# A transformer block on one core: projection and feed-forward products beside a value burst issued as four 32-column tiles, with the engine orders and banks written out as lists

## The chip, the core and the metric

The kernel runs on one core of a Trainium2 chip. The metric is device time in microseconds (us), from the first to the last instruction of one execution, the median of three runs. The engines named below are PE (TensorE, matmuls), PEld (TensorE's weight loads), ACT (ScalarE), DVE (VectorE), POOL (GpSimd) and SP (the engine that issues most DMAs).

## The reference

```python
# x: 2048 tokens x 1024; 32 query heads of 32, one key/value head (multi-query attention)
mod = (silu(c) @ w_mod)                                   # six vectors sa, ca, ga, sb, cb, gb
h = layernorm(x) * (1 + ca) + sa
q = h @ wq; k = h @ wk; v = h @ wv
p = softmax(q k^T * 32**-0.5)
x = x + ga * ((p v) @ wo)
h = layernorm(x) * (1 + cb) + sb
x = x + gb * ((silu(h @ w1) * (h @ w3)) @ w2)             # w1, w3: 1024 x 3584
```

## The kernel before, in words

**Attention.** Queries are cut into 8 blocks of 256 tokens, and the 32 heads into 8 groups of four. That makes 64 units (block, group), and each unit has 8 *steps*, one for each 256 keys: 512 steps in all. In step c the function `s_exp` issues one score burst on PE: 8 matmuls with 32 rows each, four at a time in the four row groups of the array, written `S<-QT,KT` in the profile. They fill four of the six score banks (tensor S6, `S` in the profile). Then ACT takes the exponential in two instructions of 128x1024 (`U<-S`), which write slot c mod 10 of U. The third burst back used the same banks, so that score burst c can only start once the first exponential of step c-1 is done.

When the 8 steps of a unit have their exponentials, `av` multiplies them with the values: 64 matmuls (`PB<-U,V`) of 128 rows and 32 columns, four at a time at `tile_position` (0, 0), (0, 32), (0, 64) and (0, 96), one head each. This is the *value burst*. The softmax's denominators are sums on DVE (`pairs`, `psum`: `PS<-U`, `PS<-PS`), followed by four matmuls with a matrix of ones (`md`, `PB<-PS,ONES`); DVE transposes, inverts and scales (`finish_av`).

**The rest of PE's work** consists of products with 128 rows and 128 columns: the query projection (`q_proj`, `PB<-HT,W`), the output projection (`wo`, `PB<-WO,QT`), the first feed-forward layer in 14 slabs of 256 columns per token block (`slab`, `PB<-QT,HT` and `PB<-QT,W`) and the second in four quarters (`quarter`, `PB<-W2S,HT`). Each instruction moves 256 or 512 columns of the moving operand. The feed-forward layers of token block n run during the attention of block n+1 and n+2; those of the last block run after the last step. During the attention all these products and the value burst share two PSUM banks (6 and 7, `PB`); the six score banks join them after the last exponentials. A group of nodes that fills a bank and the ones that empty it form a session (`Sess`), and the bank is free again when the last of them is done.

**The order.** `build` makes a graph of 7193 nodes, one for each small group of instructions (two 256-column products, 8 value matmuls, one DVE or ACT instruction, one DMA). Each PE node has a `mode`: "S" for a score burst, "A" for value and ones matmuls with 32 columns, "F" for the 128-column products. `Placer` (line 564) then places them: it keeps a planned time for each engine, and `choose` picks the ready node with the lowest due time, corrected by a row of the table `PLAN` (line 115) that holds for 8 steps: by how late a score burst may be, by how long value products and "F" products must stay apart after a score burst (`hold`), and by offsets per kind of node and engine. `bank_for` gives a session the bank that is free first. Within an engine instructions run in the order in which they were placed, and `emit` adds semaphore waits for the node's predecessors on other engines.

Of the kernel before, what the change touches and what calls it, by code (L numbers as in the profile page):

```python
# [8 lines left out]
P = 128  # L9
# [11 lines left out]
def play(e, call):  # L21
    return getattr(e, call[0])(*call[1], **call[2])  # L22

# [19 lines left out]
class Graph:  # L43
# [4 lines left out]
    def __init__(self, nc):  # L48
        self.nc = nc
        self.nodes = []  # L50
        self.last = {}
        self.readers = {}
        self.tag = None

    def op(self, eng, fn, dur, reads=(), writes=(), vt=0.0, mode=None, sess=None, post=0.05, waw=True, after=(),
# [27 lines left out]
        for key in writes:  # L83
            for p in self.readers.get(key, ()):
                if p is not n:
                    self._edge(p, n, False)
            if waw:
                for p in self.last.get(key, ()):
                    self._edge(p, n, True)
# [17 lines left out]
    def alias(self, new, old):  # L107
# [7 lines left out]
PLAN = [  # L115
    (0.15, 0.06, 0.0, 1, 2.5,
     {"-/pe": -103, "-/act": -50, "-/sp": 3, "an/dve": 282, "av/dve": -1, "k/pe": -256, "k/dve": -10, "kb/pe":
      -34, "kb/dve": 65, "ln/pe": -40, "ln/act": -38, "ln/dve": -35, "ln/pool": -168, "mc/dve": -131, "mc/sp":
      108, "mod/pe": 152, "mod/dve": -37, "out/sp": -203, "pair/dve": 33, "q/pe": -5, "q/dve": 85, "q/sp": 102,
      "quarter/pe": 283, "quarter/dve": -115, "quarter/sp": -6, "s/pe": -111, "s/act": 268, "slab/pe": -5,  # L120
      "slab/act": -109, "slab/dve": -124, "slab/sp": -92, "v/pe": 334, "v/dve": -2, "v/pool": 65, "wo/pool": 36,
      "wo/sp": 49}),
    (0.05, 0.0, 0.02, 1, 0.5,
     {"-/pe": -121, "-/dve": 5, "-/pool": 99, "an/dve": 28, "av/pe": -78, "av/dve": 293, "k/pe": -7, "k/dve": 5,
      "kb/pe": -3, "kb/dve": -7, "ln/pe": -135, "ln/act": -119, "ln/dve": 218, "ln/pool": 78, "mc/pe": -52,
      "mc/dve": -88, "mc/sp": 27, "mod/pe": -3, "mod/dve": -58, "pair/dve": 15, "q/pe": -194, "q/dve": 14,
      "quarter/dve": 169, "s/pe": -109, "s/act": 7, "sc/dve": -11, "slab/pe": -47, "slab/act": -3, "slab/dve":
      -201, "slab/sp": 35, "v/pe": 32, "v/dve": -164, "v/pool": 298, "wo/pe": -1, "wo/dve": 18, "wo/pool": 11,
      "wo/sp": 3}),
    (0.3, 0.16, 0.1, 0, 3.1,  # L130
     {"-/pe": -93, "-/act": 12, "-/dve": -31, "-/pool": -31, "an/dve": 150, "av/pe": 7, "av/dve": 140, "k/pe":
      32, "k/dve": 90, "kb/pe": 2, "kb/dve": -29, "ln/pe": -31, "ln/act": -6, "ln/dve": 351, "ln/pool": -30,
      "mc/pe": -4, "mc/dve": -69, "mc/sp": -137, "mod/dve": 45, "out/sp": -162, "pair/dve": 66, "q/dve": 67,
      "quarter/pe": -36, "quarter/sp": 1, "s/pe": -112, "s/act": 140, "sc/dve": -32, "slab/pe": 146, "slab/act":
      -146, "slab/dve": -120, "slab/sp": -5, "v/pe": 131, "v/pool": -72, "wo/dve": 100, "wo/pool": -3}),
    (0.12, 0.06, 0.3, 0, 3.0,
     {"-/pe": 23, "-/act": -86, "-/dve": -4, "an/dve": 63, "av/pe": -29, "av/dve": 40, "k/pe": 4, "kb/dve": -10,
      "ln/pe": -27, "ln/act": 2, "ln/pool": 220, "mc/pe": 152, "mc/dve": 120, "mc/sp": -35, "mod/pe": -220,
      "mod/dve": -16, "out/sp": -16, "q/dve": 7, "q/sp": -147, "quarter/pe": -153, "quarter/dve": -41,
      "quarter/sp": -39, "s/pe": 23, "s/act": 1, "sc/dve": 74, "slab/pe": -18, "slab/dve": 2, "slab/sp": 30,  # L140
      "v/pe": -5, "v/dve": 35, "v/pool": 168, "wo/pool": 2, "wo/sp": -85}),
    (0.12, 0.24, 0.1, 1, 0.8,
     {"-/pe": -90, "-/act": 54, "-/dve": -67, "-/pool": 131, "an/dve": 109, "av/pe": 17, "av/dve": -135,
      "k/dve": 56, "kb/dve": 4, "ln/pe": -27, "ln/act": 1, "ln/pool": -16, "mc/pe": 4, "mc/dve": 10, "mc/sp":
      -8, "mod/dve": -44, "out/sp": -171, "q/pe": -226, "q/dve": -34, "q/sp": -3, "quarter/pe": 37,
      "quarter/dve": 416, "quarter/sp": -122, "s/pe": 145, "s/act": 282, "sc/dve": -18, "slab/pe": 96,
      "slab/act": -104, "slab/dve": 17, "slab/sp": 60, "v/pool": 23, "wo/pe": -24, "wo/dve": -41, "wo/pool":
      -164, "wo/sp": -28}),
    (0.12, 0.2, 0.02, 1, 3.2,
     {"-/pe": 9, "-/act": 22, "-/dve": -30, "-/pool": 14, "an/dve": 85, "av/pe": -38, "av/dve": -130, "k/pe": 8,  # L150
      "k/dve": 63, "kb/dve": 1, "ln/pe": -5, "ln/act": 96, "ln/dve": 351, "ln/pool": -16, "mc/pe": -3, "mc/dve":
      -18, "mc/sp": -3, "mod/pe": 2, "mod/dve": -44, "out/sp": -301, "pair/dve": -20, "q/pe": -94, "q/dve": 65,
# [408 lines left out]
]  # L561


class Placer:

    SWITCH = {"F": 0.105, "S": 0.111, "A": 0.1155}
    LAT = {("dve", "pe"): 0.12, ("act", "pe"): 0.1, ("act", "dve"): 0.06}
    SEM = 0.06
    SPAN = 8

    def __init__(self, g, banks, later, plan):
# [249 lines left out]
def build(nc, x_in, wq_in, wk_in, wv_in, wo_in, w1_in, w3_in, w2_in, c_in, wmod_in, out, S, D, F):  # L821
# [803 lines left out]
    i = 0  # L1625
# [108 lines left out]
```

## Time and profile before

| what | value |
|---|---|
| median of 3 runs | 1130.08 us (1130.03 to 1130.63) |
| the profiled execution, its span | 1129.6 us, 34462 instructions |
| PE / PEld / DVE / ACT / POOL busy | 98% / 67% / 86% / 90% / 5% of the span |
| granted PE clock, mean | 0.998 |
| first score burst / last score burst / end | 30.06 / 1026.61 / 1129.6 us |
| DMA engines busy, by the queue's own packets | 66% of 16 engines' span |

The profiled execution's span stands 0.5 us under the median of the runs. Three parts follow each other: about 30 us of layer norm, transposes and first projections; about 997 us from the first score burst to the last, in which ACT works through 1024 exponentials while PE does everything else in between; and 103 us after the last score burst, in which PE works off what is left of block 6 and all of block 7.

### The profile page before, as it was taken

The numbers are of one execution on the slowest core, as the hardware profiler recorded it, in microseconds if no ns is written. First come the engines' busy times: TensorE is split into PE (matmuls) and PEld (weight loads), VectorE is DVE, ScalarE is ACT, GpSimd is POOL, SyncE is SP. The second block draws the span as 40 slices with busy tenths as digits, with TensorE's granted clock in tenths as the row PEclk, the third lists the DMA queues.
The fourth block names the chain that finished last, engine by engine and source line by source line (L and its number), as shares of the span: only waits on it lengthen the run. The fifth ranks groups of instructions, "written<-read, shape, count | busy, mean of one in ns | idle before, by whom it ended". The sixth has DMA issues, their size and how long they took to land.

```text
span 1129.6 us, 34462 instructions
## 1 busy us (share of the span) xinstructions
PE 1110.8 (98%) x15472; PEld 753.3 (67%) x15472; DVE 976.4 (86%) x1484; ACT 1017.2 (90%) x1155; POOL 51.5 (5%) x95
## 2 busy tenths in 40 slices
PE   8999999999999999999999999999999999999998
PEld 6643445666577766777577766776577756776887
DVE  7877899999899989998999899988999899987542
ACT  6899999999999999999999999999999999984110
POOL 4100000000000001000100001000100001000000
PEclk9999999999999999999999999999999999999999
DMA  9500368665697656865696577865597568677794
GB/s 345 184 2 2 113 184 225 192 183 164 141 245 203 190 141 179 243 192 155 151 269 192 166 184 179 237 193 155 129 274 207 157 172 209 195 223 217 222 249 154
DMA packets 374307, 209.45 MB, mean 185 GB/s; under 512 B 17552, under 2 KB 365968, under 8 KB 374160
## 3 DMA queue, kind: packets, MB, share of 16 engines
q1 hardware_dynamic: 373728, 207.11, 66.3%
q8 instruction: 122, 2.00, 0.8%
q14 instruction: 25, 0.20, 0.1%
q10 hardware_dynamic: 432, 0.13, 0.0%
HBM read 199.89 MB, written 4.19 MB: 181 GB/s over the span
## 4 chain that ended last, share of the span: by engine, by line
PE 73%; ACT 22%; DVE 2%; DMA 1%; issue 0%; SPq 0%; POOL 0%
PE PB L22 55%; ACT U L22 21%; PE S L22 19%; DMA W<-in_A_wq_dram 1%; ACT HT L22 1%; DVE ST L22 1%; DVE PS L22 1%; DVE HT L22 0%; SPq L22 0%; ACT XNB L22 0%; DVE KT L22 0%; DVE XNB L22 0%; POOL RS L22 0%; DVE QT L22 0%; DVE X L22 0%
## 5 line engine op out<-in xcount | busy, mean ns | idle before, releaser
L22 ACT ACTIVATE U<-S 128x1024 bf16<-128x1024 f32 x1024 | 961.7, 1154 | 7.2 <-PE S L22 5.1
L22 DVE TENSOR_TENSOR PS<-U 128x2048 bf16<-128x2048 bf16 x248 | 300.9, 1218 | 34.1 <-ACT U L22 30.9
L22 DVE TENSOR_TENSOR PS<-PS 128x1024 bf16<-128x1024 bf16 x304 | 268.3, 883 | 4.8
L22 PE MATMUL PB<-QT,W 128*128 128x256 bf16 x1824 | 226.7, 273 | 0.0
L22 PE MATMUL S<-QT,KT 32*128 32x256 bf16 x4096 | 203.7, 273 | 6.8 <-ACT U L22 3.3
L22 PEld LDWEIGHTS PB<-QT,W 128*128 128x128 bf16 x1824 | 167.5, 98 | 45.7 <-issue 27.6
L22 PE MATMUL PB<-W2S,HT 128*128 128x256 bf16 x1512 | 187.5, 273 | 0.0
L22 PEld LDWEIGHTS PB<-W2S,HT 128*128 128x128 bf16 x1512 | 138.2, 98 | 39.4 <-issue 23.6
L22 PEld LDWEIGHTS S<-QT,KT 32*128 32x128 bf16 x4096 | 60.8, 92 | 141.6 <-ACT U L22 137.7
L22 PE MATMUL PB<-U,V 128*32 128x256 bf16 x4096 | 132.3, 273 | 0.6 <-DVE QT L22 0.6
L22 PE MATMUL PB<-QT,HT 128*128 128x256 bf16 x928 | 117.0, 273 | 0.0
L22 PEld LDWEIGHTS PB<-U,V 128*32 128x32 bf16 x4096 | 105.7, 97 | 12.9 <-issue 8.0
L22 PE MATMUL PB<-HT,W 128*128 128x256 bf16 (+1 forms) x576 | 103.3, 320 | 1.1 <-DVE QT L22 0.5
L22 PEld LDWEIGHTS PB<-QT,HT 128*128 128x128 bf16 x928 | 85.4, 98 | 22.7 <-issue 13.3
L22 DVE SCALAR_TENSOR_TENSOR HT<-HT,PB 128x512 bf16<-128x512 bf16 x100 | 68.4, 684 | 18.0 <-ACT HT L22 17.6
L22 ACT ACTIVATE HT<-PB 128x512 bf16<-128x512 f32 (+1 forms) x102 | 71.4, 701 | 9.0 <-PE PB L22 8.2
L22 PEld LDWEIGHTS PB<-HT,W 128*128 128x128 bf16 x576 | 50.2, 98 | 38.8 <-issue 14.6
L22 DVE TENSOR_TENSOR HT<-HT,PB 128x512 bf16<-128x512 bf16 x100 | 68.2, 682 | 4.3 <-PE PB L22 3.1
L22 ACT ACTIVATE HT<-S 128x512 bf16<-128x512 f32 (+1 forms) x16 | 11.1, 702 | 59.7 <-PE S L22 59.6
L22 POOL TENSOR_SCALAR RS<-MV 128x1 f32<-128x1 f32 x32 | 14.2, 445 | 968.8 <-DVE MV L22 968.8
L22 PE MATMUL PB<-WO,QT 128*128 128x512 bf16 x224 | 55.4, 381 | 0.0
L22 PEld LDWEIGHTS PB<-WO,QT 128*128 128x128 bf16 x224 | 18.8, 97 | 24.6 <-issue 7.2
(119 smaller groups left out, 699.4 us busy)
## 6 DMA issues: line engine op xcount, KB each, us to landing
W<-in_B_w_dram SPq DMA_DIRECT2D x150, 512.0 KB, 5.0
W2S<-in_B_w_dram SPq DMA_DIRECT2D x28, 1792.0 KB, 8.3
HT<-in_B_w_dram SPq DMA_DIRECT2D x74, 512.0 KB, 5.0
W2S<-in_w_mod_dram SPq DMA_DIRECT2D x8, 1024.0 KB, 7.4
X<-in_A_x_dram SPq DMA_DIRECT2D x8, 512.0 KB, 6.6
out_dram<-X SPq DMA_DIRECT2D x7, 512.0 KB, 9.6
U<-in_B_w_dram SPq DMA_DIRECT2D x1, 3584.0 KB, 18.3
W2S<-in_B_w_dram SPq DMA_DIRECT2D x1, 3584.0 KB, 12.7
```

The lines of the kernel that those rows point to most:

```text
L22: return getattr(e, call[0])(*call[1], **call[2])
```

## The change

**Lists in place of the planner.** `Placer` and `PLAN` are gone. The class `Ordered` takes from the table `ORDER`, for each engine, the list of node numbers in the order in which it is to issue them, and from the string `BANKS` the bank of each session. It fixes nothing else: waits are still added from the graph's edges.

**Column tiles.** `Ordered.run` cuts PE's list at the score bursts. Where a piece between two score bursts holds at least one "A" node, all "F" nodes of that piece are marked (`narrow`), and `emit` passes their calls through `column_tiles`: each matmul with 128 weight columns and at least 256 moving columns becomes four matmuls with 32 weight columns each, which write 32 partitions each of the same bank, at the same four tile positions as the value burst. The piece after the last score burst holds the last value burst, so that all products after it are marked as well.

**Graph edges.** A write that does not order itself behind the last writer (`waw=False`) now keeps the edges that the first writer had.

```diff
+def column_tiles(calls):
+    r = []
+    for name, (dst, w, x), k in calls:
+        if name != "matmul" or w.shape[-1] != P or dst.shape[0] != P or len(w.shape) != 2 or x.shape[-1] < 256:
+            return calls
+        for h in range(4):
+            q = slice(32 * h, 32 * (h + 1))
+            r.append((name, (dst[q], w[:, q], x), dict(k, tile_position=(0, 32 * h))))
+    return r
...
         for key in writes:
-            for p in self.readers.get(key, ()):
-                if p is not n:
-                    self._edge(p, n, False)
+            before = [(p, False) for p in self.readers.get(key, ()) if p is not n]
             if waw:
-                for p in self.last.get(key, ()):
-                    self._edge(p, n, True)
+                before += [(p, True) for p in self.last.get(key, ())]
+                self.before[key] = before
+            else:
+                before += self.before.get(key, [])
+            for p, strong in before:
+                self._edge(p, n, strong)
...
-PLAN = [
-    (0.15, 0.06, 0.0, 1, 2.5,
...
+ORDER = {
+    "pe": """
+        31-35 23 36-47 25 48-52 65 53-57 28 27 105 122-132 74 133-137 96 76-77 148 168 177 113 157 115-118 107 195 108
...
+BANKS = (
+    "6676776677767767776767666667666776767776767767676767776677676676676777676776677667676666766767676776"
...
+        step = []
+        for i in self.order["pe"] + [None]:
+            if i is None or nodes[i].mode == "S":
+                if any(nodes[k].mode == "A" for k in step):
+                    self.narrow.update(k for k in step if nodes[k].mode == "F")
+                step = []
+            else:
+                step.append(i)
...
+        if e == "pe":
+            calls = [(c, a, dict(k, skip_group_check=True) if c == "matmul" else k) for c, a, k in calls]
+            if n.i in self.narrow:
+                calls = column_tiles(calls)
...
-    pl = Placer(G, (6, 7), later, PLAN)
+    pl = Ordered(G, (6, 7), later, ORDER, BANKS)
```

Three places of PE's order are shown. In the rows, the last figures are the size of what one instruction writes, partitions x columns: an "F" product that writes 32 partitions is one of the four tiles. The first place is steps 262 to 267, around the value burst of one unit. Before, the burst stands in one step, with nothing else:

```order
L22 MATMUL S<-QT,KT 128x256 x8
L22 MATMUL PB<-W2S,HT 128x256 x12
L22 MATMUL S<-QT,KT 128x256 x8
L22 MATMUL PB<-W2S,HT 128x256 x12
L22 MATMUL S<-QT,KT 128x256 x8
L22 MATMUL PB<-PS,ONES 32x256 x4
L22 MATMUL PB<-U,V 32x256 x64
L22 MATMUL S<-QT,KT 128x256 x8
L22 MATMUL PB<-W2S,HT 128x256 x12
L22 MATMUL S<-QT,KT 128x256 x8
L22 MATMUL PB<-W2S,HT 128x256 x12
```

In the change, the same steps 263 to 267 on PE:

```order
L22 MATMUL S<-QT,KT 128x256 x8
L22 MATMUL PB<-W2S,HT 128x256 x14
L22 MATMUL S<-QT,KT 128x256 x8
L22 MATMUL PB<-W2S,HT 32x256 x32
L22 MATMUL PB<-PS,ONES 32x256 x4
L22 MATMUL PB<-U,V 32x256 x16
L22 MATMUL S<-QT,KT 128x256 x8
L22 MATMUL PB<-U,V 32x256 x48
L22 MATMUL S<-QT,KT 128x256 x8
L22 MATMUL PB<-W2S,HT 128x256 x12
```

The burst is spread over two steps, and 8 products of the second feed-forward layer stand in the first of them as 32 instructions. The second place is PE's rows at the first score burst (after the last bias products, `PB<-SAB,W`). Before:

```order
L22 MATMUL PB<-SAB,PS 128x16 x8
L22 MATMUL PB<-SAB,W 128x16 x16
L22 MATMUL PB<-HT,PS 128x256 x24
L22 MATMUL S<-QT,KT 128x256 x8
L22 MATMUL PB<-HT,PS 128x256 x8
```

And in the change, the same place:

```order
L22 MATMUL PB<-SAB,PS 128x16 x8
L22 MATMUL PB<-SAB,W 128x16 x16
L22 MATMUL PB<-HT,PS 128x256 x12
L22 MATMUL S<-QT,KT 128x256 x8
L22 MATMUL PB<-HT,PS 128x256 x12
```

Twelve of the key and query projections' products have moved behind the first score burst. The third place is the beginning of PE's rows after the last score burst. Before:

```order
L22 MATMUL S<-QT,KT 128x256 x8
L22 MATMUL PB<-W2S,HT 128x256 x30
L22 MATMUL PB<-PS,ONES 32x256 x4
L22 MATMUL PB<-U,V 32x256 x64
L22 MATMUL S<-W2S,HT 128x256 x14
L22 MATMUL S<-PS,ONES 32x256 x4
L22 MATMUL S<-W2S,HT 128x256 x28
L22 MATMUL S<-WO,QT 128x512 x32
```

In the change:

```order
L22 MATMUL S<-QT,KT 128x256 x8
L22 MATMUL PB<-W2S,HT 32x256 x8
L22 MATMUL S<-WO,QT 32x512 x24
L22 MATMUL PB<-W2S,HT 32x256 x120
L22 MATMUL S<-PS,ONES 32x256 x4
L22 MATMUL S<-U,V 32x256 x64
L22 MATMUL S<-PS,ONES 32x256 x4
L22 MATMUL S<-W2S,HT 32x256 x120
L22 MATMUL S<-WO,QT 32x512 x24
```

All products are tiles there, and some of the output projection has moved ahead of the last value burst.

913 lines of the change are left out of this document (311 added, 602 removed), and 3 rows, old and new, of the table ORDER.

## The prediction

> **What bounds the kernel now.** I read the busy times by stretch first, cut at four score bursts that the timeline gives: the first, those of step 64 and step 488, and the last. (The columns are the stretch, its length, then busy time and instructions of PE, PEld, DVE, ACT, POOL, the granted clock and the DMA share.)
>
> ```profile
> 30.06 0.40 PE L22 MATMUL S<-QT,KT 32*128 32x256 bf16 x8
> 150.86 0.40 PE L22 MATMUL S<-QT,KT 32*128 32x256 bf16 x8
> 975.84 0.40 PE L22 MATMUL S<-QT,KT 32*128 32x256 bf16 x8
> 1026.61 0.40 PE L22 MATMUL S<-QT,KT 32*128 32x256 bf16 x8
> 30.06:150.86 120.80, 117.24 (x1857) 59.27 (x1858) 99.98 (x181) 117.35 (x128) 4.76 (x11) 0.99 0.25 82
> 150.86:975.84 824.98, 818.35 (x11616) 551.73 (x11617) 765.43 (x1112) 823.77 (x939) 30.53 (x40) 1.00 0.71 190
> 975.84:1026.61 50.77, 50.70 (x707) 37.26 (x708) 44.42 (x62) 46.49 (x55) 0.00 (x0) 1.00 0.66 187
> ```
>
> In the long middle stretch ACT is busy for 823.77 of 824.98 us, and PE for 818.35. The two are nearly level there: what PE saves can only shorten it as far as ACT's own pace allows. Next the chain of waits, which gives both paces:
>
> ```profile
> 135.12 53.35 ACT U L22 x58
> 211.09 6.42 ACT U L22 x7
> 1102.23 24.47 PE S L22 x224
> ```
>
> An exponential takes 6.42/7 = 0.917 us on ACT (53.35/58 = 0.920), hence a step of two 1.83 us. A 128-column product of 256 moving columns takes 24.47/224 = 0.109 us on PE. The tanh of a slab adds 0.49 us to ACT, the distance of these two starts in ACT's timeline:
>
> ```profile
> 188.37 0.60 ACT L22 ACTIVATE HT<-PB 128x512 bf16<-128x512 f32 x1
> 188.86 4.68 ACT L22 ACTIVATE U<-S 128x1024 bf16<-128x1024 f32 x5
> ```
>
> PE's own cost of a step is read from the timeline of a step that mixes both forms of work:
>
> ```profile
> 403.56 0.40 PE L22 MATMUL S<-QT,KT 32*128 32x256 bf16 x8
> 403.89 0.62 PE L22 MATMUL PB<-U,V 128*32 128x256 bf16 x16
> 404.44 1.05 PE L22 MATMUL PB<-W2S,HT 128*128 128x256 bf16 x8
> 405.42 0.40 PE L22 MATMUL S<-QT,KT 32*128 32x256 bf16 x8
> ```
>
> From the score burst to the next form of work 0.33 us pass; the 8 products then take 0.98 us to the next burst, that is 8 x 0.109 + 0.11, and the 16 value matmuls, taken as four groups of four, 0.55 = 4 x 0.109 + 0.11. Each change of form thus costs about 0.1 us. A step with one form and n products (a group of four value matmuls counts as one product, 512 columns as two) costs PE 0.44 + 0.109 n us. Twelve products make 1.75 us and fit ACT's 1.83; 13 make 1.86 and don't, unless a tanh stands in the step.
>
> **Part 1, the column tiles themselves.** The change issues the same arithmetic in four times the instructions. The nearest row is the value burst, which has the very form of a tile: own weights of 128x32, 256 moving columns, four positions.
>
> ```profile
> 1026.94 3.45 PE L22 MATMUL PB<-W2S,HT 128*128 128x256 bf16 x30
> 1030.44 1.92 PE L22 MATMUL PB<-U,V 128*32 128x256 bf16 x64
> L22 PE MATMUL PB<-W2S,HT 128*128 128x256 bf16 x1512 | 187.5, 273 | 0.0
> L22 PE MATMUL PB<-U,V 128*32 128x256 bf16 x4096 | 132.3, 273 | 0.6 <-DVE QT L22 0.6
> L22 PEld LDWEIGHTS PB<-U,V 128*32 128x32 bf16 x4096 | 105.7, 97 | 12.9 <-issue 8.0
> ```
>
> One matmul lasts 0.273 us, so that 30 products start every (3.45 - 0.273)/29 = 0.1096 us, and 16 groups of four every (1.92 - 0.28)/15 = 0.109 us. I take 0 for the price of a tiled product. The order holds 682 tiled products in 104 steps and 868 after the last step, 1550 in all. The bound above: the group rows give 4 x 132.3/4096 = 0.1292 us for a group of four and 187.5/1512 = 0.1240 for a product. Their 5 ns come mostly from the ends of shorter runs; as a rate they are 1550 x 0.0052 = 8.1 us. The bound below is 0 too: no row shows a tile group faster than 0.109.
>
> The Trainium skill, TensorEngine Tiling (Array Packing), Feature Incompatibilities, says that column tiling excludes Fast Weight Load, and TensorE: Matmul & The Clock Gate, LDWEIGHTS, gives columns/1.2 ns for a plain load: 27 ns for 32 columns, 107 ns for four. By that the loads of a tiled product would just fit the 109 ns; the trace agrees for the value burst, where 64 loads fit into its 1.92 us, and shows no tile of a 128-column weight.
>
> **Part 2, changes of form.** Before, 43 of the 511 whole steps mix value matmuls and 128-column products, now 2 (the others that mix are all tiles). 41 x 0.1 = 4.1 us of PE's time go. That is time of PE, and ACT's pace covers most of it, so it enters through part 3 alone.
>
> **Part 3, the steps.** With the prices above I added up PE's and ACT's work for every block of eight steps (from the orders of both kernels) and took the larger of the two in each block. All blocks: PE 973.1 us before (511 x 0.44 + 6813 products x 0.1092 + 43 x 0.1) and 971.0 after (6831 products, 2 changes); ACT 984.7 in both (1022 exponentials, 98 tanhs). By stretch, the sums of the larger:
>
> - steps 0 to 63: before 117.9, after 118.3; the trace took 120.80.
> - steps 64 to 487: before 826.1, after 824.1; the trace took 824.98.
> - steps 488 to 510: before 50.8, after 51.3; the trace took 50.77.
>
> The account hits the last two within 1.1 us, so I use its differences: -2.0 and +0.5. In the middle stretch the gain cannot exceed 824.98 - 821.8 (ACT's work there: 848 x 0.9165 and the tanhs) = 3.2 us.
>
> In steps 0 to 63 the trace lost 2.9 us beyond the account. ACT's timeline shows where:
>
> ```profile
> 30.51 5.61 ACT L22 ACTIVATE U<-S 128x1024 bf16<-128x1024 f32 x6 [1.96 <-PE S L22]
> 36.83 1.94 ACT L22 ACTIVATE U<-S 128x1024 bf16<-128x1024 f32 x2 [0.72 <-PE S L22]
> 39.27 5.61 ACT L22 ACTIVATE U<-S 128x1024 bf16<-128x1024 f32 x6 [0.50 <-PE S L22]
> 132.76 1.94 ACT L22 ACTIVATE U<-S 128x1024 bf16<-128x1024 f32 x2 [0.81 <-PE S L22]
> 135.12 5.60 ACT L22 ACTIVATE U<-S 128x1024 bf16<-128x1024 f32 x6 [0.41 <-PE S L22]
> 132.20 0.69 DVE L22 TENSOR_SCALAR XNB<-PB 128x512 bf16<-128x512 f32 x1 [0.96 <-PE PB L22]
> ```
>
> At 132 us two matmuls of the modulation's gate (`PB<-XNB,ONES`) and their evacuation on DVE stand in PE's way in steps 51 and 53. The change has them in steps 48 and 52, each first in its step. I give half of the 2.9 back (1.45), between none and all: with the account's +0.4 the stretch comes out at 118.3 + 1.45 = 119.8, 1.0 shorter.
>
> **Part 4, the start.** The first score burst waits behind 24 products (timeline: a key tile's evacuation, then PE):
>
> ```profile
> 27.02 3.11 PE L22 MATMUL PB<-HT,PS 128*128 128x256 bf16 x24
> 28.07 0.47 ACT L22 ACTIVATE KT<-S,QKB 128x256 bf16<-128x256 f32 x1 [1.24 <-DVE QKB L22]
> 28.94 0.47 DVE L22 TENSOR_SCALAR QT<-S,QKB 128x256 bf16<-128x256 f32 x1
> ```
>
> Its inputs are there at 28.5 (keys) and 29.4 (queries), and DVE's order in the change takes the query evacuation right behind the bias. Twelve products fewer ahead are 12 x 0.109 = 1.3 us: I take -1.3. It is 0 if DVE's layer norms set the eighth key tile, which no order makes shorter, and -2.5 if the inputs, now loaded in another order by SP (five loads of x first), come sooner as well.
>
> **Part 5, after the last score burst.** PE runs dense there (for its last 224 products the chain names PE alone). 904 products stand there before, 894 after: -10 x 0.109 = -1.1 us. The forms change four times in both (before around the ones and value matmuls, after around the transposes). If the output projection's norm, now covered by 42 products as before, came late, up to 1 us would come back.
>
> The sum: -1.0 - 2.0 + 0.5 - 1.3 - 1.1 = **-4.9 us**, against the profiled 1129.6 us, so 1124.7; the runs' median stands 0.5 us higher, so 1130.08 - 4.9 = **1125.2 us**.
>
> **The rivals.**
>
> *Tiles are dearer than the value burst shows (slower).* A value burst has one weight slice for all four positions and four moving operands; a tiled product has four weight slices and one moving operand. If that costs the 5.2 ns of part 1, the 868 tiles at the end lie wholly on the path, and the 682 others stand in steps whose PE work is the longest. All of it is +8.1, and 1125.2 + 8.1 = 1133.3 us. It decides from 4.9/1550 = 3.2 ns a product (no gain left). For it: no row shows such a product. Against: PE's and PEld's rows are the same for both forms, 0.273 and 97 to 98 ns.
>
> *The written list waits (slower).* Each hand-over of the two banks to DVE that comes late costs about what it costs now:
>
> ```profile
> PEld PB L22 <- DVE PS L22: 5.5, 26, 0.2
> ```
>
> 0.2 us each. One more in each of the 64 units is 12.8 us, and 1125.2 + 12.8 = 1138 us. Against: DVE's work between the pair sums is spread more evenly in the change (added up from its order with the spacing of its back-to-back rows, 1.14 us for a pair sum: the heaviest 16 steps hold 29.1 us where it was 30.4, and those around step 52 28.5 for 33.4).
>
> *Nothing moves.* The step blocks' -2.0 and the start's -1.3 are swallowed by ACT's pace and DVE's layer norms: -1.1 + 0.5 - 1.0 = -1.6, that is 1128.5 us.
>
> *ACT's floor.* All three stretches come down to ACT's own work (117.3, 821.8 and 45.6): 996.6 - 984.7 = 11.9 less, with start and end 14.3, that is 1115.8 us. Against: the last stretch's 51.3 on PE.
>
> **How the numbers follow.** A measurement here can tell about 0.2%, 2.3 us, from no change. The forecast has 0.53, ACT's floor (or well towards it) 0.08, nothing moves 0.13, dearer tiles 0.18, a waiting list 0.08. Faster by over 0.2% is the first two, 0.61; within 0.2% 0.13; slower is the last two, 0.26. The forecast's own range is 1125.2 with part 1 at 0, the middle between -3.2 and 0, the early loss and start between 0 and -5.4: about 1121 to 1129. For 8 in 10 I reach to 1119 (half way to the floor) and to 1134 (the dear tiles); outside are the floor itself and the waiting list.
>
> **What would show it.** Right: in the timeline after, 16 or more tiled products in a row start every 0.109 us; ACT busy for over 99.8% from step 64 to 488 in about 823 us; first score burst near 28.8; about 101.9 us from the last burst to the end. Wrong: the last stretch grows although it holds 10 products fewer (dearer tiles), or waits of PE's loads on DVE grow from 0.2 us x 26 to some tens of us (the list waits).

## The result: 3.9% slower, and the profile after

The changed kernel took 1175.88 us (median of 5 runs, 1170.38 to 1176.6) against 1130.19 (1130.03 to 1131.38) for the kernel before in the same session: a ratio of 1.0391, 95% interval 1.0374 to 1.0407. The forecast of 1125.2 us was wrong by 51 us and in its sign, and none of its rivals had the cause.

The windows view of the changed kernel, cut at the same four score bursts and at the end, and below it the stretch after the last burst of the kernel before (columns as in the prediction: length, then busy time and instructions of PE, PEld, DVE, ACT, POOL, the granted clock, the DMA share):

```profile
28.33:149.24 120.91, 118.28 (x2041) 63.66 (x2040) 103.39 (x187) 117.64 (x129) 5.27 (x12) 1.00 0.26 88
149.24:996.66 847.42, 820.05 (x13259) 558.39 (x13257) 748.78 (x1106) 826.68 (x940) 29.46 (x42) 0.99 0.68 185
996.66:1047.92 51.26, 51.26 (x775) 37.53 (x774) 43.27 (x60) 47.08 (x55) 0.00 (x0) 1.00 0.65 186
1047.92:1172.87 124.95, 104.60 (x3465) 96.76 (x3464) 43.16 (x77) 10.73 (x17) 1.59 (x4) 0.97 0.64 185
```

```profile
1026.61:1129.60 102.99, 99.64 (x943) 85.38 (x942) 43.97 (x78) 10.97 (x17) 1.59 (x4) 1.00 0.81 223
```

The first burst comes 1.7 us earlier, steps 0 to 63 take 0.1 longer, the middle 22.4 longer, steps 488 to 510 0.5 longer, the end 22.0 longer: together the 43.3 us by which the span grew. That the medians differ by 45.7 lies in the kernel before: its profiled execution has a mean granted clock of 0.998, as 8 of its 23 runs beside experiment 12 (1131.3 to 1133.1 us), while the other 15 show 1.000 (1129.9 to 1130.6). In the last stretch PE has nothing to wait for but its own stream, and yet it is busy for only 104.60 of 124.95 us. What it waits for are the first two rows of PE's waits after (engine, what it writes, what ended the wait: total us, times, longest; over the whole kernel). The second fence is the first row of the same view of the kernel before, where no row of PE names "issue":

```profile
PE PB L22 <- issue: 16.2, 10, 3.3
PE S L22 <- issue: 16.1, 13, 3.1
PE S L22 <- ACT U L22: 8.2, 16, 1.4
```

```profile
PE S L22 <- ACT U L22: 3.3, 9, 0.8
```

"issue" is idle time in which PE waited for nothing that the profile shows. In the last stretch it comes to 17.2 us in 12 stops, and the view lists no other wait of PE there. The timeline of PE in the last stretch shows one such place, and a long run of tiles:

```profile
1068.50 1.25 PE L22 MATMUL PB<-W2S,HT 128*32 128x256 bf16 x37
1072.63 0.29 PE L22 MATMUL PB<-W2S,HT 128*32 128x256 bf16 x3 [2.87 <-issue]
...
1077.76 1.93 PE L22 MATMUL PB<-W2S,HT 128*32 128x256 bf16 x64
```

In the run, 64 tiles take 1.93 us; the value burst's 64 matmuls took 1.92. So the tile itself costs what the prediction said. But between 1068.50 and 1072.63 PE stands still for 2.87 us in the middle of one bank's products, with no dependency shown at that place.

The places have a pattern. Counted along PE's instructions (matmuls, weight loads and the few semaphore instructions between them), the ten longest stops after the last burst come at numbers 33729, 33985, 34241, 35521, 36033, 36545, 36801, 37825, 38081 and 38337. All differ by multiples of 256. The DMA queues' rows, first of the changed kernel and then of the one before, hold a queue of kind "instruction" (packets, MB, share of 16 engines):

```profile
q8 instruction: 156, 2.56, 0.9%
```

```profile
q8 instruction: 122, 2.00, 0.8%
```

2.56 MB in 156 packets is 16 KB a packet. The 34 more packets go with 8820 more recorded matmuls and loads on PE (39764 where there were 30944), about 259 for a packet. In the stop shown, PE starts the last instruction of a block at 1069.48 us; the packet of that queue runs from 1070.07 to 1071.19, and PE goes on at 1072.63. In all ten stops PE goes on 1.3 to 1.6 us after a packet's end (two later ones: ends at 1137.84 and 1144.59, PE at 1139.33 and 1146.09).

So the theory, called FETCH from here on: PE's instructions arrive in blocks of 256. A product in the old form is two instructions in 0.109 us, and a block lasts 14 us. As four tiles it is eight instructions, 13.6 ns each, and a block lasts 3.5 us; PE then runs out of instructions before the next block is there. The Trainium skill, Runtime: NRT & Kernel Launch, Instruction fetch mechanics, describes 16 KiB blocks of 256 instructions that the sequencer fetches through a DMA queue of its own, and the packets here agree. It adds that the fetch is hidden by the pace at which instructions are issued; the rows above show that it isn't at 13.6 ns an instruction.

A second thing follows some of the longer stops. The windows row from 1073.90 to 1077.20, 1.3 us behind the stop shown, has a granted clock of 0.50, and the same 8 transposes take 1.03 us inside it and 0.63 behind it:

```profile
1073.90:1077.20 3.30, 3.30 (x52) 2.09 (x44) 1.84 (x4) 0.00 (x0) 0.00 (x0) 0.50 0.00 0
```

```profile
1075.26 1.03 PE L22 MATMUL S<-IDENT,XNB 128*128 128x128 bf16 x8
1077.20 0.63 PE L22 MATMUL S<-IDENT,XNB 128*128 128x128 bf16 x8
```

Up to the last instructions, the records of the granted clock show 0.5 in seven stretches, six of 3.41 us and one of twice that, each after a time in which PE stood still or nearly so. Not every stop is followed by one: behind the stop of 2.05 us at 842 us the clock stayed, and the stretches at 176 and 316 us follow idle time that has nothing to do with instructions (experiment 1 has both). A stretch of 3.41 us at half the clock costs PE up to 1.7 us, an estimate from its length.

### The profile page after: what moved, and what is told of

Read it like the earlier page. It is cut to its first block, busy times and chain, and to the rows that moved or that the text cites. A ratio compares the mean times of both kernels' runs of the same rounds, so it can differ in the third digit from the quotient of the medians.

```text
span 1172.9 us, 43325 instructions
## 1 busy us (share of the span) xinstructions
PE 1117.1 (95%) x19882; PEld 775.0 (66%) x19882; DVE 960.1 (82%) x1480; ACT 1021.0 (87%) x1156; POOL 51.6 (4%) x98
## 3 DMA queue, kind: packets, MB, share of 16 engines
q8 instruction: 156, 2.56, 0.9%
## 4 chain that ended last, share of the span: by engine, by line
ACT 48%; PE 43%; DVE 4%; issue 3%; DMA 0%; POOL 0%; DVEq 0%
ACT U L22 46%; PE PB L22 31%; PE S L22 12%; ACT HT L22 2%; DVE PS L22 2%; DVE ST L22 1%; DVE HT L22 0%; DVE X L22 0%; DMA X<-in_A_x_dram 0%; DVE RB L22 0%; DVE QT L22 0%; DVE XNB L22 0%; POOL PS L22 0%; DVE MV L22 0%; ACT PS L22 0%
## 5 line engine op out<-in xcount | busy, mean ns | idle before, releaser
L22 ACT ACTIVATE U<-S 128x1024 bf16<-128x1024 f32 x1024 | 957.7, 1078 | 25.4 <-PE S L22 25.1
L22 PE MATMUL PB<-QT,W 128*128 128x256 bf16 (+1 forms) x2812 | 244.3, 274 | 5.3 <-issue 3.8
L22 PEld LDWEIGHTS PB<-QT,W 128*128 128x128 bf16 (+1 forms) x2812 | 178.4, 97 | 51.0 <-issue 31.2
L22 PE MATMUL PB<-W2S,HT 128*128 128x256 bf16 (+1 forms) x2522 | 205.2, 277 | 4.9 <-issue 4.9
L22 PEld LDWEIGHTS PB<-W2S,HT 128*128 128x128 bf16 (+1 forms) x2522 | 149.7, 98 | 44.7 <-issue 28.8
L22 PE MATMUL PB<-QT,HT 128*128 128x256 bf16 (+1 forms) x1392 | 120.9, 275 | 3.8 <-issue 2.6
L22 PEld LDWEIGHTS PB<-U,V 128*32 128x32 bf16 x4032 | 101.6, 97 | 23.5 <-issue 18.3
L22 PEld LDWEIGHTS PB<-QT,HT 128*128 128x128 bf16 (+1 forms) x1392 | 85.9, 98 | 26.1 <-issue 15.8
L22 PE MATMUL PB<-HT,W 128*128 128x256 bf16 (+3 forms) x720 | 102.5, 322 | 0.2
L22 PEld LDWEIGHTS PB<-HT,W 128*128 128x128 bf16 (+1 forms) x720 | 50.8, 97 | 35.6 <-issue 13.1
L22 PE MATMUL PB<-WO,QT 128*128 128x512 bf16 (+1 forms) x316 | 59.0, 381 | 0.7 <-DVE HT L22 0.2
L22 PEld LDWEIGHTS PB<-WO,QT 128*128 128x128 bf16 (+1 forms) x316 | 20.1, 97 | 25.0 <-issue 6.5
## 6 DMA issues: line engine op xcount, KB each, us to landing
W2S<-in_B_w_dram SPq DMA_DIRECT2D x1, 3584.0 KB, 16.8
```

## The experiments

Times are medians; a ratio is to the kernel before on the same chip. "End" is the time after the last score burst.

**1. No tiles at all.** The written lists stay.

```diff
-                if any(nodes[k].mode == "A" for k in step):
+                if False and any(nodes[k].mode == "A" for k in step):
```

> The change's written order and banks, with no product cut into tiles (the marked list stays empty). Two theories. FETCH: the order is sound, and what costs is that the tiles raise PE's instruction rate to 8 instructions in 0.109 us, so that a block of 256 instructions lasts 3.5 us and the next block is not there in time; PE then idles at block ends (10 + 13 idle times put down to issue, 32 us together). Without tiles these idle times go, and what comes back is 126 more changes of form at 0.1 us of PE's time, which by the account of eight-step blocks make the steps 5.6 us longer (999.3 for 993.7): 1129 to 1136 us. ORDER: the written list itself waits (banks, DVE), tiles or not: 1160 us or more. No tile price of its own can be told from FETCH by this run.

1139.13 us, ratio 1.0073 (1.0056 to 1.0089). The windows of the middle and the end:

```profile
150.01:985.53 835.52, 821.46 (x11549) 544.11 (x11546) 749.44 (x1106) 829.42 (x940) 28.43 (x42) 0.99 0.69 187
1037.17:1138.72 101.55, 98.58 (x939) 84.81 (x938) 42.90 (x77) 10.73 (x17) 1.59 (x4) 1.00 0.77 225
```

The end is 101.55 us, where the prediction had 101.9. So 37 us of the loss go with the tiles, and without them the written order is 9 us slower than the planner's. This lies 3 us above FETCH's range.

**2. Tiles only between score bursts.**

```diff
-                if any(nodes[k].mode == "A" for k in step):
+                if i is not None and any(nodes[k].mode == "A" for k in step):
```

> Tiles only between score bursts (682 products); the 868 after the last score burst are issued whole. FETCH: the idle times at block ends after the last score burst go, and the end is as long as its 894 products say, 102 us instead of 125: 1151 to 1155 us. DEARER TILES (a price for each tiled product of 44/1550 = 28 ns, without regard to blocks): 868 x 28 ns = 24 us less, 1150 us, too, but then the 104 steps with tiles are longer evenly, by 0.2 us each, where FETCH has a few idle times of 1.5 to 3.5 us, 256 instructions apart or a multiple of it.

1150.52 us, ratio 1.0175 (1.0145 to 1.0204), half a us under FETCH's range; end 101.14. The whole loss of the end went with its tiles; the steps keep theirs. PE's waits:

```profile
PE PB L22 <- issue: 13.2, 8, 3.6
PE S L22 <- issue: 4.9, 4, 2.1
```

Of these 18.1 us 16.2 stand in the middle, in 10 stops, and their instruction numbers (5056, 12737, 15296, ..., 30658) leave the same remainder by 256, within two: the few long pieces of FETCH, not the even growth of DEARER TILES.

**3. The end in two tiles of 64 columns, the steps unchanged.**

```diff
-def column_tiles(calls):
+def column_tiles(calls, width=32):
...
-        for h in range(4):
-            q = slice(32 * h, 32 * (h + 1))
+        for h in range(P // width):
+            q = slice(width * h, width * (h + 1))
...
-                    self.narrow.update(k for k in step if nodes[k].mode == "F")
+                    self.narrow.update((k, 64 if i is None else 32) for k in step if nodes[k].mode == "F")
```

> As the change, but after the last score burst each product is cut into two tiles of 64 columns instead of four of 32: still column tiles, with half the instructions. FETCH: a block of 256 instructions lasts 7 us there, the next one is in time, the idle times go: the end takes 102 to 104 us and the whole 1151 to 1156 us. DEARER TILES (column tiling itself slows weight loads or matmuls): the end keeps at least half of its 22 us, 1163 us or more.

1149.52 us, ratio 1.0168 (1.0141 to 1.0196). The end's windows row:

```profile
1042.20:1143.86 101.66, 98.75 (x1781) 94.55 (x1780) 42.95 (x77) 10.72 (x17) 1.59 (x4) 1.00 0.78 226
```

Column tiles at 27 ns an instruction cost nothing: 101.66 us, no stop. It is not the cut of the array into columns that is dear. (The whole is 1.5 us under the range.)

**4. The weights of the end cut away.** Of the last block's slabs an eighth is loaded from the fourth slab on, of its second layer a twenty-eighth; the rest is left out.

```diff
+            if n == NB - 1 and s >= 3:
+                dst, src = dst[:, 0:1, :], src[:, 0:1, :]
...
-            dma("sp", W7[h], w2_in[:, h * 512:(h + 1) * 512].rearrange("(c p) f -> p c f", p=P), ("W7", h),
+            dma("sp", W7[h][:, 0:1], w2_in[:, h * 512:(h + 1) * 512].rearrange("(c p) f -> p c f", p=P)[:, 0:1], ("W7", h),
```

> As the change, with tiles everywhere, but the weight loads of the last block's slabs 3 to 13 and of its second layer fetch an eighth and a twenty-eighth of their data (the rest of the weights is left out). FETCH has two forms. QUEUE: the instruction blocks come late because their packets stand behind weight packets on the DMA engines; with the weights gone the end falls to 102 to 108 us, the whole to 1152 to 1160. LATENCY: a block needs about 3.5 us from its request whatever else is moved; the end stays above 118 us, the whole above 1166 us.

1158.87 us, ratio 1.0247 (1.0215 to 1.0279). The end's row:

```profile
1052.07:1160.73 108.66, 102.86 (x3465) 96.54 (x3464) 43.03 (x77) 10.73 (x17) 1.59 (x4) 0.98 0.21 55
```

The same instructions, 108.66 us instead of 124.95. With the DMA share down from 0.64 to 0.21, 16 of the 23 us are gone: the blocks come late mostly because of the weights' traffic. The end is 0.7 us over QUEUE's range, the whole within it. Seven us stay, of which 2.3 are stops named "issue".

The packets of the instruction queue tell what the traffic stretches. One packet takes 1.06 us on average in the end of the changed kernel and 1.12 here, so it isn't the transfer. What differs is when it starts. Counted from the moment when PE passes a block's end, the next packet starts 4.1 to 4.3 us later ahead of the changed kernel's stops at 1065.87, 1072.63, 1139.33 and 1146.09 us, and 1.1 us later in a typical place here, with PE at the same pace (the end passed at 1111.0, the packet from 1112.1). Ahead of each of the ten stops read above the packet began only after PE had passed the end before; that fits a store of about one block ahead, and not a long one. What a packet stands behind until it starts is not in the records.

**5. Two tiles of 64 columns everywhere** (32 becomes 64 and four becomes two in `column_tiles`).

> The changed kernel with every tiled product cut into two matmuls of 64 columns, in the steps as well as after the last burst. FETCH (PE's instructions arrive in blocks of 256 and a run of four 32-column tiles uses a block up in 3.5 us): half the instructions, a block lasts 7.0 us, as in the end of the third experiment, which had no stall; so no stall in the steps either beyond the 8 us of idle time that the kernel without tiles has, end 101.6 us, and 1128 to 1136 us in all. FORM (the gain of the tiles in the steps lies in their form being that of the value matmuls, and a change between 64 and 32 columns costs 0.1 us like any other): the 122 changes of the kernel without tiles come back, 1137 to 1141 us. TILES (it is the writing of part of the partitions that costs, not the fetch): 1145 us or more.

1144.38 us, ratio 1.011 (1.0095 to 1.0125). The end is 101.6 and no stop shows, but the middle takes 838.3 us, not less than without tiles. A step of its timeline shows why: between the value matmuls of 32 columns and the tiles of 64 there is a change of form again. Twelve groups of value matmuls at 0.109 us make 1.31, and the tiles start 1.42 after them; the two tiled products take 0.35 where 0.22 would do.

```profile
564.34 1.49 PE L22 MATMUL PB<-U,V 128*32 128x256 bf16 x48
565.76 0.41 PE L22 MATMUL PB<-W2S,HT 128*64 128x256 bf16 x4
566.11 0.40 PE L22 MATMUL S<-QT,KT 32*128 32x256 bf16 x8
```

FORM had it right in kind, but 1144.38 is 3 us over its 1137 to 1141; FETCH's 1128 to 1136 was missed. The time alone would leave TILES (1145 or more) open, as it is only 0.6 us under; the end speaks against it, where every product is cut into tiles and 101.63 us is what it takes without them.

**6. The kernel before, with its planner, and tiles only in sessions that begin after the last burst.**

```diff
+        if self.step < 512 and n.sess is not None:
+            n.sess.allow = None
+        if e == "pe" and n.mode == "F" and self.step == 512 and n.sess.allow is not None:
+            calls = [(c, a, dict(k, skip_group_check=True) if c == "matmul" else k) for c, a, k in calls]
+            calls = column_tiles(calls)
```

> The kernel before, with its own order, and only the products of the sessions that begin after the last score burst cut into four 32-column tiles. FETCH: everything up to the last burst as before (1026.6 us), the end grows from 103.0 to 121 to 126 us as in the changed kernel, so 1148 to 1153 us. ORDER (the end of the changed kernel is long because of what the written lists put there, and the tiles only add to it): end below 110 us, 1130 to 1137 us.

1155.03 us, ratio 1.0214 (1.0196 to 1.0232). Its end, and its waits of PE:

```profile
1025.38:1152.32 126.94, 105.33 (x3391) 93.78 (x3390) 43.95 (x78) 10.96 (x17) 1.59 (x4) 0.98 0.63 184
```

```profile
PE S L22 <- issue: 12.7, 11, 3.7
PE PB L22 <- issue: 4.5, 3, 2.2
```

Up to the last burst the kernel is as before (1025.38 us where the profiled execution before had 1026.61), and the end grows from 102.99 to 126.94 us, a little over the range. The waits named "issue", 17.2 us, all lie in the end. The long end has nothing to do with the written lists. The stops stand at instruction numbers that leave the same remainder by 256 (29889, 31426, 31682, ..., 34498, within one).

**7. Three tiles a product in the end: 64, 32 and 32 columns.**

```diff
-        for h in range(4):
-            q = slice(32 * h, 32 * (h + 1))
+        for lo, hi in ((0, 64), (64, 96), (96, 128)):
+            q = slice(lo, hi)
```

> The changed kernel without tiles in the steps, and after the last burst three tiles a product, of 64, 32 and 32 columns: six instructions with the loads in 0.109 us or 18 ns each, between 13.6 ns (end of 124.9 us) and 27 ns (101.7 us, no stall). FETCH: a block of 256 lasts 4.65 us; a block takes about 1.1 us to arrive, 1.5 us until PE goes on, and waits for the weights' packets before, so stalls remain but shorter and fewer: end 104 to 116 us, in all 1141 to 1153. TILES (a cost of each 32-column tile): half of the tiles are gone, end 101.6 + 23.4/2 = 113 us and spread evenly over the products, not in pieces at multiples of 256 instructions.

1423.18 us, ratio 1.2584 (1.256 to 1.2608): all three theories missed, and the run says nothing about FETCH. The end takes 385.2 us. Its timeline:

```profile
1099.93 1.84 PE L22 MATMUL PB<-W2S,HT 128*64 128x256 bf16 x12
1101.70 0.51 PE L22 MATMUL S<-W2S,HT 128*64 128x256 bf16 x3
```

The 12 matmuls are four products; the next one starts 1.77 us later, 0.443 us a product. Tiles of different width don't run side by side. In the trace the two tiles of 32 start 3 ns apart, but 0.227 us after the one of 64, and the next tile of 64 starts 0.216 us after them: twice the 0.109 us of a group, plus two changes of form of about 0.11 each. It is the same price as the prediction's 0.1 between value matmuls and products. The Trainium skill, TensorEngine Tiling (Array Packing), Key Properties, says that a change of the tiling mode drains TensorE; these starts agree.

**8. No tiles, and the empty steps filled.** In PE's list of experiment 1, the value nodes 1363 to 1366 move from steps 73 and 74 into the empty steps 76 and 78, and the product nodes 1317 to 1321 from steps 147 and 148 into 148 and 149.

> The changed kernel without tiles, with PE's list altered at two places where steps stand empty: in the second block's first units 8 value products move from steps 73 and 74 into the empty steps 76 and 78, and further on 10 products of the second feed-forward layer move from step 147 to 148 and 149. CLOCK (PE's idle time there makes the clock drop to half for 3.4 us at a time, at 176 us for 6.8 us and at 316 us for 3.4 us): the two stretches are gone, and the middle part falls from 835.5 by 3 to 7 us; 1132 to 1136 us in all. FORM (what the order without tiles loses is the 122 changes of form at 0.1 us, 4.5 us by the account, wherever they stand): 1138 to 1140 us, as without the move.

1140.26 us, ratio 1.0077 (1.0062 to 1.0093); experiment 1 had 1.0073. The middle fell by 1.2 us, not by 3 to 7. The stretch at half clock at 316 us went away, the one at 176 us stayed, although PE idled less in those steps, first in experiment 1 and then here:

```profile
173.85 0.40 PE L22 MATMUL S<-QT,KT 32*128 32x256 bf16 x8 [1.44 <-ACT U L22]
```

```profile
173.51 0.40 PE L22 MATMUL S<-QT,KT 32*128 32x256 bf16 x8 [0.89 <-ACT U L22]
```

So the stretch at 316 us cost 1.2 us. What the one at 176 us costs (up to 3.4 us, by its 6.83 us at half the clock) this run doesn't show, since it stayed; experiments 2 and 10 have it too.

**9. As many instructions in the end without any column tile:** each product is cut along its moving operand into four matmuls of a quarter of the columns, with the whole 128x128 weights; no tiles in the steps.

```diff
-        for h in range(4):
-            q = slice(32 * h, 32 * (h + 1))
-            r.append((name, (dst[q], w[:, q], x), dict(k, tile_position=(0, 32 * h))))
+        m = x.shape[-1] // 4
+        for h in range(4):
+            q = slice(m * h, m * (h + 1))
+            r.append((name, (dst[:, q], w, x[:, q]), k))
```

> The changed kernel without column tiles anywhere; after the last score burst each product is cut along its moving operand instead, into four matmuls of 64 columns (128 of 512) with the whole 128x128 weights. As many instructions as with four column tiles, in the same 0.109 us, but nothing of a tile: FETCH expects the same stalls in pieces of 1 to 3 us at places that differ by multiples of 256 instructions, and an end of 118 to 128 us, 1155 to 1166 us in all. TILES (the cost comes of the array's cut into columns): an end of 101.5 to 105 us without such pieces, 1139 to 1143 in all. Should a load of whole weights not fit in the 27 ns of 64 columns, the end grows evenly in both, to what the spacing of a run shows times 894.

1167.0 us (two runs), ratio 1.0318 (1.0284 to 1.0353), 1 us over FETCH's range. The end, and the waits of PE:

```profile
1037.48:1161.81 124.33, 107.08 (x3465) 104.86 (x3464) 43.36 (x77) 10.74 (x17) 1.59 (x4) 1.00 0.64 187
```

```profile
PE S L22 <- issue: 11.3, 12, 2.6
PE PB L22 <- issue: 5.5, 6, 2.0
```

3465 matmuls and 3464 loads, as many as with tiles, and an end of 124.33 us, as long as with tiles, with no tile in it. It is 22.8 us longer than the end of experiment 1. Of the 16.8 us in the two rows 14.3 lie in the end, at numbers with one remainder by 256, within one. Most of the rest is even, as a run of 79 of these matmuls and a single one show:

```profile
1047.76 2.46 PE L22 MATMUL S<-W2S,HT 128*128 128x64 bf16 x79 [0.32 <-issue]
...
1058.22 0.19 PE L22 MATMUL PB<-W2S,HT 128*128 128x64 bf16 x1
```

(2.46 - 0.19)/78 is 29.1 ns each, 0.116 us a product instead of 0.109, and 868 products make 6 us of that; about 2 us are left over. With experiment 3 (tiles, fewer instructions, no loss) this settles it for the end: the number of instructions is the cause.

**10 and 11. Nearly all feed-forward loads cut,** with tiles in the steps (10, on experiment 2) and without (11, on experiment 1). The stale weights are used; the rest is left out.

```diff
+            if n * NSLAB + s >= NW:
+                dst, src = dst[:, 0:1, :], src[:, 0:1, :]
...
+        k = NF if n == 0 and q < 2 else 2
-        dma("sp", W2S[:, r], w2_in[:, q * 256:(q + 1) * 256].rearrange("(c p) f -> p c f", p=P), ("W2S", r),
+        dma("sp", W2S[:, r, 0:k], w2_in[:, q * 256:(q + 1) * 256].rearrange("(c p) f -> p c f", p=P)[:, 0:k], ("W2S", r),
```

> The second experiment (column tiles in the steps alone) with nearly all loads of feed-forward weights cut: of each slab's weights an eighth is loaded after the first three slabs, of the second layer's a fourteenth after the first two quarters and a twenty-eighth for the last block; the rest of the weights is left out and stale values are used. QUEUE (a block of instructions comes late because its packet stands behind the weights' packets): the stalls in the steps shrink from 24.6 us to the 4 to 10 that the other kernels have for other reasons, the middle part from 851.0 to 823 to 832 us, as was predicted for it, and the whole comes to 1125 to 1135 us. LATENCY (a block takes its 2.6 us however empty the queues are, and PE outruns it anyway): the middle stays above 842 us and the whole above 1143.

> The first experiment (no tiles) with the same loads cut, as the control: its steps have no waits for instructions, so FORM (what it loses against before is the 122 changes of form and two stretches at half clock, all on PE) expects the same time as without the cut, 1136 to 1140 us with the middle at 833 to 836. If part of that loss was also fetch or memory traffic, the middle falls below 831 us.

10 took 1129.86 us, ratio 0.9992 (0.9982 to 1.0001); 11 took 1140.13, ratio 1.0084 (1.0067 to 1.0101). The middle of experiment 2, of 10 and of 11:

```profile
149.15:1000.15 851.00, 820.89 (x13259) 558.47 (x13258) 748.99 (x1106) 826.44 (x940) 29.47 (x42) 0.99 0.68 184
```

```profile
149.16:974.64 825.48, 810.82 (x13259) 554.45 (x13257) 747.57 (x1106) 824.11 (x940) 29.36 (x42) 1.00 0.15 41
```

```profile
149.82:984.55 834.73, 821.21 (x11549) 543.86 (x11547) 749.54 (x1106) 829.25 (x940) 29.36 (x42) 0.99 0.15 40
```

With the DMA share down to 0.15, the tiles' middle falls from 851.00 to 825.48 us, and without tiles it hardly moves (835.52, 834.73). PE's waits named "issue" in 10 are one row of 1.6 us where experiment 2 had 18.1:

```profile
PE PB L22 <- issue: 1.6, 2, 1.0
```

QUEUE holds in the steps as in the end: 10 falls in its range, and 11 is at the upper edge of FORM's. The pair also gives the worth of the tiles when instructions arrive in time: 834.73 - 825.48 = 9.25 us for 111 changes of form fewer in these steps (112 and 1, counted from the orders), at most 0.083 us each. At most, because 11 has the stretch at half clock at 316 us and 10 hasn't, which experiment 8 puts at 1.2 us; without that it is 0.073.

**12 and 13. The written start, the old rest.** All engines follow the changed kernel's lists up to score burst 61 and the order before from there on; in 12 the steps up to there keep their tiles (144 matmuls), in 13 there are none.

```diff
-                if any(nodes[k].mode == "A" for k in step):
+                bursts += 1
+                if bursts <= 62 and any(nodes[k].mode == "A" for k in step):
```

> Written lists joined from both kernels: all engines follow the changed kernel's lists up to score burst 61 (with its column tiles in the steps up to there, 144 tile matmuls in all), and from there on the order of the kernel before, without tiles; three score bursts at the joint are moved forward so that no step there stands empty. In the changed kernel burst 60 came 1.7 us earlier than before, and no wait for instructions stands ahead of it. START (that lead is real and nothing after it takes it back): the steps from 64 on take 824 to 826 us, the last stretch 50.8, the end 103, so that the whole is 1.0 to 1.9 us under the kernel before, ratio 0.9983 to 0.9991. SWALLOWED (the order before has slack in its first 80 steps that waits for something else, so that a lead is lost there): ratio 0.9995 to 1.0005.

> The same joined lists without any column tile. FORM (each change of form spared by the tiles is worth 0.1 us on PE in the steps up to 61, where PE bounds): burst 60 comes 0.7 to 0.9 us later than with tiles, and the whole 0.2 to 0.9 us under the kernel before, ratio 0.9992 to 0.9999. If tiles do nothing there, the ratio is that of the joined lists with tiles.

12: 1131.91 us, ratio 1.0014 (1.0005 to 1.0023). 13: 1131.52 us, ratio 1.0011 (1.0002 to 1.002). In 12 both theories are missed by a little on the slow side. In 13 FORM is missed too; that the tiles do nothing there (the ratio of 12) fits. In the profiled execution of 12 a lead is there (burst 60 1.5 us earlier, and every burst from 64 to the end 1.56 us earlier). But it is a lead over the profiled execution before, whose clock fell once, and the execution, at 1129.85 us, was the quickest of twelve, which went up to 1135.62. Its span of 1128.1 us is no shorter than that of the runs before at a clock of 1.000 (1128.1 to 1128.7): so as a whole the kernel gains nothing over those. In 13's, the lead of 2.3 us at burst 9 is a delay of 1.7 at burst 12. The timeline there, in 13:

```profile
48.44 0.38 PE L22 MATMUL PB<-IDENT,PS 128*128 128x128 bf16 x4 [1.56 <-issue]
```

The granted clock is 0.5 for 3.41 us from 48.76 on, right behind this stop; the changed kernel has the same stop and no fall of the clock there. So the delay of 13 is not the changes of form alone, and its one profiled execution can't price them. No version here that does the whole work beats the kernel before.

## Why the prediction was wrong, point by point

**Part 1, the price of a tiled product (0): the step that failed, by about 45 us (21.9 in the middle, 847.42 - 825.48 of experiment 10, and 23.4 at the end, 124.95 - 101.55 of experiment 1).** Its reading of the array was right: 64 tiles in 1.93 us, and 64-column tiles for nothing. What it didn't ask is what feeds PE. The value burst that it took as the nearest row is 64 matmuls and 64 loads, 128 instructions, half a block; it stands between score bursts and waits and can't show what a stream of such instructions does over several blocks. The upper bound of 8.1 us came from the same rows. Experiments 2, 3, 6 and 9 show it for the end, 10 for the steps. The price is not one per product, as the term has it, but a stop at the end of a block that was used up too soon, and now and then a stretch at half clock behind it: of the 21.9 us in the middle 13.2 are stops, of the 23.4 at the end 17.2. The figures of the stretches are from single executions (the same steps took 841.95 us in experiment 3 and 851.00 in experiment 2); the medians give 25.4 us from the changed kernel to experiment 2 and 20.7 from there to 10, about the same.

**Part 2, changes of form (0.1 us each): right.** 0.07 to 0.08 us in the steps (10 against 11), about 0.11 between widths (7). The prediction set the 2 changes of the tiled order against before's 43; what it didn't say is that the written order needs the tiles: without them it has 128 changes, 85 more than before, and is 9 us slower (experiments 1 and 11).

**Part 3, the middle (-2.0): hidden, then short.** With the fetch out of the way it is +0.5 (825.48 against 824.98), ACT being busy for 824.11 us of it, the forecast's 99.8%. So the 2.0 us were not there even so; ACT was as good as full in both. The stretch at half clock at 174 us, 6.83 us long, which the kernel before hasn't, may have taken a part; no run shows how much.

**Part 3, steps 0 to 63 (-1.0): +0.1.** The account had no term for instructions here either. Bursts 3 to 9 come 2.7 to 3.7 us earlier than before, and at burst 12 only 0.3 is left. The timeline of the changed kernel in between:

```profile
44.74 0.95 PE L22 MATMUL PB<-PS,HT 128*128 128x32 bf16 x32
45.62 0.40 PE L22 MATMUL S<-QT,KT 32*128 32x256 bf16 x8
45.95 0.40 PE L22 MATMUL PB<-IDENT,PS 128*128 128x128 bf16 x4
47.91 0.38 PE L22 MATMUL PB<-IDENT,PS 128*128 128x128 bf16 x4 [1.56 <-issue]
```

The value projection's 32 short matmuls (with the loads, 64 instructions in about 0.9 us) stand right ahead of a block's end: instruction 1473, the same remainder by 256 as the stops of the end. This stop is in every kernel with the written start, tiles or not. It accounts for 1.56 of the 2.55 us lost between bursts 9 and 12; the rest wasn't traced.

From burst 48 to 56 the changed kernel gains 1.55 us, about the 1.45 that was given back there, but not for the reason given. The prediction put the loss at 132 us down to the gate's two matmuls. The rows of the kernel before say something else:

```profile
129.85 1.89 PE L22 MATMUL PB<-HT,W 128*128 128x512 bf16 x4
131.53 0.63 PE L22 MATMUL PB<-XNB,ONES 128*128 128x128 bf16 x4
132.65 2.09 PE L22 MATMUL PB<-HT,W 128*128 128x512 bf16 x8
134.67 0.40 PE L22 MATMUL S<-QT,KT 32*128 32x256 bf16 x8
```

Four products of 512 columns take 1.68 us to the next row, and right behind them eight take 2.02: the granted clock is 0.5 from 129.65 to 133.06 us, in this one execution. The changed kernel has no such stretch there. Most runs of the kernel before, at a clock of 1.000, can't have it either, so against them the gain is mostly luck of the execution that was profiled.

**Steps 488 to 510 (+0.5): right,** 51.26 us where 51.3 stood. **Part 4, the start (-1.3): right in kind,** -1.72. **Part 5, the end without the tiles' price (101.9): right,** 101.55 in experiment 1.

**The rivals.** *Dearer tiles* had the right side and the wrong mechanism: it looked for the cost in the array and at 5.2 ns a product, and its own sign, a last stretch that grows with fewer products, came true for another reason. *The written list waits* named a slower order, but not its way: its own sign failed (PEld's waits on DVE's `PS` fell from 5.5 to 2.4 us), and the 9 us of the order without tiles are mostly changes of form. Neither reached 1170. *Nothing moves* (1128.5 us) comes nearest to what is left without the fetch's price: experiment 10, with no tiles in its end and light loads, took 0.9992 of the kernel before.

Two things stay open. The granted clock's fall to 0.5 behind idle time is seen in the records; by how much PE must idle for it was not settled (experiment 8 filled 0.55 us of each step and the clock still fell; behind the same stop of 1.56 us at 48 us it fell in experiment 13 and not in the changed kernel). And the runs of 12 and 13 spread over 4 to 6 us. In 12 this goes with the clock (1129.9 to 1131.6 us at a mean of 0.997, 1131.6 to 1135.6 at 0.994 and 0.995); where it falls was not traced, since only one execution of each was profiled.

## What to carry to other kernels

Before cutting an instruction into several, count the instructions, not only the array's time: divide the instructions of the densest stretch by its length and compare it with what the fetch has been seen to sustain (here the dense ends ran at 256 instructions in 4.6 to 4.8 us under full weight traffic, in 4.0 with the traffic cut, and were free of stops at 7.3). A short burst in the profile is no price for a long stream of the same instruction; look for a row that is longer than a block, 256 instructions here. "issue" among the waits of a busy engine, at instruction numbers with one remainder by 256, is the sign.

## What the runs showed of the hardware that was not expected

- PE's instruction stream is slowed by the kernel's own loads. The same 6929 matmuls and loads of the end took 124.95 us at a DMA share of 0.64 and 108.66 at 0.21, while a packet took 1.06 and 1.12 us: the traffic delays its start, not its transfer.
- In the ten stops PE went on 1.3 to 1.6 us after the packet's end, which comes on top of the packet's 1.1 us.
- Matmuls of 128 weight columns and 64 moving columns run every 29.1 ns with their loads, hardly slower than 256 columns in one piece (0.116 against 0.109 us a product).
- Column tiles of 64 and of 32 columns, on different columns of the array, don't run side by side: 0.443 us a product.
